# A load that waits for seven eighths of the store ahead of it, and stores cut 56 to 8, in a scaled residual add

## The chip, the core and the metric

The kernel runs on one core of a Trainium2 chip. A core has a matrix engine (TensorE, PE in the profile), a vector engine (VectorE, DVE), a scalar engine, GpSimd (POOL) and SyncE (SP), which here only issues transfers and waits. Each engine works through its own list of instructions in order; semaphores tie the lists together. Data is moved between the main memory (HBM) and the on-chip memory (SBUF, 128 partitions) by 16 DMA engines. The metric is the device time of one launch in microseconds (us). The time before is 152.25 us, the median of 3 runs (152.24 to 152.48).

## The reference

```python
B, S, D = 512, 32, 640          # x, fx: (512, 32, 640) bf16, alpha: (1,) bf16

def reference(x, fx, alpha):
    return x + alpha * fx
```

Each of x, fx and the output has 10,485,760 elements of two bytes, 20.97 MB. So 41.94 MB are read and 20.97 MB are written.

## The kernel before

Each tensor is seen as 128 partitions of 81,920 contiguous elements. A partition's row is counted in units of K = 512 elements (1 KB), so a tensor is 160 units wide, and one unit over all partitions is 131,072 bytes. The row is worked through in three pieces (line 18): units 0 to 64, 64 to 128 and 128 to 160. They are called p0, p1 and p2; the parts of fx, x and the output that belong to them are f0, x0 and the first store; f1, x1 and the second store; f2, x2 and the third.

On the chip there are three slots of 64 units each, a, b and c (line 42). f0 goes to slot a, x0 to b, f1 to c. x1 goes to slot a again, once f0 has been used up, and f2 and x2 share slot b (lower and upper half), once the first store has read it.

The order is written out by hand (`manual_schedule`, line 40): each engine does its work in the order of the lines, and the framework adds only the waits that the data needs. All transfers, loads and stores alike, are issued by SyncE in `move` (lines 45 to 48), so they go through one queue in the order of the calls: f0's first 8 units, its other 56, alpha, x0, f1, the first store, x1, f2, x2, the second store, the third. The three waits on that list that matter here are these. The first store (line 87) waits for its addition. x1's load (line 88) needs slot a, which the addition on line 85 has read by then, so it is issued right behind the first store. f2 (line 90) needs slot b and so waits until the first store has landed; x2 follows it at once.

VectorE does two kinds of steps, in place. `scaled` (line 61) multiplies a piece of fx by alpha, which a small matrix product has spread over the 128 partitions (lines 73 to 80); `added` (line 64) adds the scaled piece to the piece of x. Its order is: scale f0, add into x0, scale f1, add into x1, scale f2, add into x2. Each addition of a 64-unit piece is one instruction, and the store behind it waits for the whole of it.

The last instruction on SyncE (lines 97 to 100) waits for everything but the third store.

Of the kernel before, what the change touches and what calls it, by code (L numbers as in the profile page):

```python
# [1 line left out]

# [4 lines left out]

ALU = mybir.AluOpType
F32 = mybir.dt.float32

K = 512
P = 128

WIDE = 64
PIECES = [(0, 64), (64, 128), (128, 160)]
HEAD = 8


@with_exitstack
def kernel(
    ctx: ExitStack,
    tc: tile.TileContext,
    x: bass.AP,
    fx: bass.AP,
    alpha: bass.AP,
    out: bass.AP,
):  # L30
    nc = tc.nc
    xv = x.flatten_outer_dims().rearrange("(p n) d -> p (n d)", p=P)
    fxv = fx.flatten_outer_dims().rearrange("(p n) d -> p (n d)", p=P)
    ov = out.flatten_outer_dims().rearrange("(p n) d -> p (n d)", p=P)
    assert xv.shape[1] == PIECES[-1][1] * K

    consts = ctx.enter_context(tc.tile_pool(name="consts", bufs=1))
    psum = ctx.enter_context(tc.tile_pool(name="psum", bufs=1, space=bass.MemoryType.PSUM))
    slots = ctx.enter_context(tc.tile_pool(name="slots", bufs=1))
    ctx.enter_context(tc.manual_schedule())  # L40

    slot = [slots.tile([P, WIDE * K], x.dtype, name=f"slot_{n}") for n in "abc"]
    done = []

    def move(out, in_):
        r = nc.sync.dma_start(out=out, in_=in_)  # L46
        done.append(r)
        return r

    def load(of, piece, at, cut=0):  # L50

        a, b = piece
        n, where = at
        t = slot[n][:, where * K : (where + b - a) * K]
        if cut:
            move(t[:, : cut * K], of[:, a * K : (a + cut) * K])
        move(t[:, cut * K :], of[:, (a + cut) * K : b * K])
        return t

    def scaled(f):  # L60
        done.append(nc.vector.tensor_scalar(out=f, in0=f, scalar1=a_f[:], scalar2=None, op0=ALU.mult))  # L61

    def added(xt, f):
        done.append(nc.vector.tensor_tensor(out=xt, in0=xt, in1=f, op=ALU.add))  # L64

    def store(piece, t):
        a, b = piece
        move(ov[:, a * K : b * K], t)

    p0, p1, p2 = PIECES  # L70
    f0 = load(fxv, p0, (0, 0), cut=HEAD)

    a_1 = consts.tile([1, 1], alpha.dtype, name="a_1")
    move(a_1[:], alpha[None, :])
    ones = consts.tile([1, P], alpha.dtype, name="ones")
    nc.vector.memset(ones[:], 1.0)  # L76
    a_ps = psum.tile([P, 1], F32, name="a_ps")
    done.append(nc.tensor.matmul(a_ps[:], ones[:], a_1[:], start=True, stop=True))  # L78
    a_f = consts.tile([P, 1], F32, name="a_f")
    nc.vector.tensor_copy(out=a_f[:], in_=a_ps[:])  # L80

    x0 = load(xv, p0, (1, 0))
    scaled(f0)
    f1 = load(fxv, p1, (2, 0))
    added(x0, f0)
    scaled(f1)
    store(p0, x0)
    x1 = load(xv, p1, (0, 0))
    added(x1, f1)
    f2 = load(fxv, p2, (1, 0))  # L90
    x2 = load(xv, p2, (1, WIDE // 2))
    scaled(f2)
    store(p1, x1)
    added(x2, f2)
    store(p2, x2)

    rest = nc.sync.nop(nofuse=True)
    info = mybir.DependencyInfo(mybir.DependencyClass.Sync, mybir.DependencyReason.DATA)
    for i in done[:-1]:
        tc.add_manual_dep(rest.ins, i.ins.name, info, reason="all but the last store")  # L100


# [1 line left out]
_INS = ['x', 'fx', 'alpha']  # L104
_OUTS = [((512, 32, 640), 'bfloat16')]


# [23 lines left out]
```

## Time and profile before

| | us |
|---|---|
| time, median of 3 runs | 152.25 |
| the profiled run | 152.39 |
| its span in the profile | 150.6 |
| VectorE busy | 65.4 (43% of the span) |
| addition over 64 units | 17.22 |
| scaling of 64 units | 8.75 |
| addition over 32 units | 8.69 |
| scaling of 32 units | 4.48 |
| a SyncE issue | 0.33 to 0.52 |

The span is the time from the first to the last instruction of the profiled execution; the run's own time has 1.79 us around it. The page counts 1442 DMA packets and 62.92 MB, a mean of 418 GB/s over the span. VectorE's waits before a step are 10.2 us for x0, 2.1 for f1 and 31.8 for x1.

Three views are used below. The timeline gives start and length of each instruction, its engine, line and operands, and in brackets how long its engine had been idle and what ended that. A transfer stands in it only with its issue on SyncE; the table of issues has the time from there to landing, which is when all 16 engines have reported the end. In the table of windows, each line is one stretch: its bounds, its length, the busy time and number of instructions of PE, PEld, DVE and POOL, the granted clock of TensorE, the DMA share (the summed time of the packets that start in the stretch, over 16 times its length) and the GB/s of those packets. As a packet is booked whole where it starts, a short stretch can have a share over 1. A packet here is what one engine moves of one partition's row, so 65,536 bytes for a piece of 64 units, 8192 for 8 units.

### The profile page before, as it was taken

Reading aid. Unit: us, or ns where it says so; the run is one execution under the profiler, and the core shown is the slowest. Engines: PE = TensorE matmul, PEld = TensorE weight load, DVE = VectorE, ACT = ScalarE, POOL = GpSimd, SP = SyncE. Lnnn points to the kernel's source line nnn. Section 1 sums busy time; section 2 is a strip of 40 time slices with the busy share of each in tenths; the row PEclk is TensorE's granted clock in tenths of the full one; section 3 lists DMA queues with packets and bytes.
Section 4 is the critical chain, followed back from the end, with each engine's and each line's share of the span. In section 5 each row is a group of like instructions: output and inputs, shape, how many; then the busy total and the mean of one; then the engine's idle time right before and its main releaser. Section 6 shows DMA issues by size and latency. Waiting matters only on the chain.

```text
span 150.6 us, 74 instructions
## 1 busy us (share of the span) xinstructions
PE 0.2 (0%) x1; PEld 0.1 (0%) x1; DVE 65.4 (43%) x8; POOL 0.2 (0%) x4
## 2 busy tenths in 40 slices
PE   0000000000000000000000000000000000000000
PEld 0000000000000000000000000000000000000000
DVE  0000009930099996895000000009999999900000
POOL 0000000000000000000000000000000000000000
DMA  5995996998969696998978999979999969898993
GB/s 174 592 487 244 487 522 278 557 470 366 557 278 557 278 557 278 557 487 348 557 278 348 470 435 418 470 331 418 426 435 435 548 278 557 366 470 383 435 418 157
DMA packets 1442, 62.92 MB, mean 418 GB/s; under 512 B 162, under 2 KB 162, under 8 KB 162
## 3 DMA queue, kind: packets, MB, share of 16 engines
q1 hardware_dynamic: 1442, 62.92, 97.6%
HBM read 41.94 MB, written 20.97 MB: 418 GB/s over the span
## 4 chain that ended last, share of the span: by engine, by line
DMA 54%; DVE 27%; issue 5%; SPq 1%; DVEq 0%
DMA slot_a<-in_x_dram 28%; DMA slot_b<-in_x_dram 26%; DVE slot_b L64 17%; DVE slot_a L64 6%; DVE slot_b L61 3%; SPq L46 1%; DVEq L64 0%
## 5 line engine op out<-in xcount | busy, mean ns | idle before, releaser
L64 DVE TENSOR_TENSOR slot_a<-slot_a,slot_c 128x32768 bf16<-128x32768 bf16 x1 | 17.2, 17224 | 31.8 <-DMA slot_a<-in_x_dram 31.8
L64 DVE TENSOR_TENSOR slot_b<-slot_b,slot_a 128x32768 bf16<-128x32768 bf16 x1 | 17.2, 17224 | 10.2 <-DMA slot_b<-in_x_dram 10.2
L61 DVE TENSOR_SCALAR slot_c<-slot_c,a_f 128x32768 bf16<-128x32768 bf16 x1 | 8.8, 8754 | 2.1 <-DMA slot_c<-in_fx_dram 2.1
L80 DVE COPY a_f<-a_ps 128x1 f32<-128x1 f32 x1 | 0.2, 159 | 21.5 <-PE a_ps L78 21.5
L61 DVE TENSOR_SCALAR slot_a<-slot_a,a_f 128x32768 bf16<-128x32768 bf16 x1 | 8.8, 8754 | 0.0
L64 DVE TENSOR_TENSOR slot_b<-slot_b 128x16384 bf16<-128x16384 bf16 x1 | 8.7, 8693 | 0.0
L61 DVE TENSOR_SCALAR slot_b<-slot_b,a_f 128x16384 bf16<-128x16384 bf16 x1 | 4.5, 4479 | 0.0
L76 DVE MEMSET ones<- 1x128 bf16 x1 | 0.2, 165 | 0.8 <-PEq L115 0.8
L78 PE MATMUL a_ps<-a,ones 1*128 1x1 bf16 x1 | 0.2, 158 | 22.3 <-DMA a<-in_alpha_dram 22.3
L115 POOL MEMSET const-bfloat16-1.0<- 128x1 bf16 x1 | 0.1, 101 | 0.0
L115 POOL MEMSET const-uint8-127<- 128x1 uint8 x1 | 0.1, 101 | 0.0
L78 PEld LDWEIGHTS <-ones 1*128 1x128 bf16 x1 | 0.1, 100 | 1.0 <-DVE ones L76 1.0
L115 POOL MEMSET const-float32-0.0<- 128x1 f32 x1 | 0.1, 98 | 0.2 <-issue 0.2
L115 POOL MEMSET const-float32-1.0<- 128x1 f32 x1 | 0.1, 98 | 0.0
## 6 DMA issues: line engine op xcount, KB each, us to landing
slot_a<-in_fx_dram SPq DMA_DIRECT2D x1, 7168.0 KB, 21.0
slot_b<-in_fx_dram SPq DMA_DIRECT2D x1, 4096.0 KB, 29.9
slot_b<-in_x_dram SPq DMA_DIRECT2D x1, 4096.0 KB, 39.3
out_dram<-slot_b SPq DMA_DIRECT2D x1, 4096.0 KB
slot_a<-in_fx_dram SPq DMA_DIRECT2D x1, 1024.0 KB, 4.6
a<-in_alpha_dram SPq DMA_DIRECT2D x1, 0.0 KB
slot_b<-in_x_dram SPq DMA_DIRECT2D x1, 39.5
slot_c<-in_fx_dram SPq DMA_DIRECT2D x1, 58.5
```

The source lines that it names most:

```text
L46: r = nc.sync.dma_start(out=out, in_=in_)
L61: done.append(nc.vector.tensor_scalar(out=f, in0=f, scalar1=a_f[:], scalar2=None, op0=ALU.mult))
L64: done.append(nc.vector.tensor_tensor(out=xt, in0=xt, in1=f, op=ALU.add))
L76: nc.vector.memset(ones[:], 1.0)
L78: done.append(nc.tensor.matmul(a_ps[:], ones[:], a_1[:], start=True, stop=True))
L80: nc.vector.tensor_copy(out=a_f[:], in_=a_ps[:])
L115: nc = _bacc.Bacc("TRN2", target_bir_lowering=False, num_devices=1)
```

## The change

The order of the steps moves from calls to a text, `PLAN`, which a loop reads line by line; the three slots become one tile, `room`, whose places are given in units (0, 64 and 128 are the old slots a, b and c). `f` and `x` are loads and `s` is a store, each with the units in the tensor and, after `@`, the place in `room`; `a` spreads alpha; `m` scales, with place and width; `+` adds, with the places of x and f and the width. `room` is 207 units wide, of which 192 are used.

Three things differ in what is issued. The first store goes as units 0 to 56 and 56 to 64. x1's load has an added wait: it is issued when the first of these two stores has landed. The addition into x1 and the second store go as 56 and 8 units. f2's load follows x1's with no wait of its own, and x2's waits for the second part of the first store, whose place it takes. Pieces, places, the order of the loads and VectorE's order are otherwise those of before.

```diff
-WIDE = 64
-PIECES = [(0, 64), (64, 128), (128, 160)]
-HEAD = 8
+PLAN = """
+f 0 8 @ 0
+f 8 64 @ 8
+a
+x 0 64 @ 64
+m 0 64
+f 64 128 @ 128
++ 64 0 64
+m 128 64
+s 0 56 @ 64
+s 56 64 @ 120
+x 64 128 @ 0 after s 0
++ 0 128 56
++ 56 184 8
+f 128 160 @ 64
+x 128 160 @ 96
+m 64 32
+s 64 120 @ 0
+s 120 128 @ 56
++ 96 64 32
+s 128 160 @ 96
+"""
...
+    def transfer(what, a, b, at, after):
+        away, here = units(whole[what], a, b), units(room, at, at + b - a)
+        out, in_ = (away, here) if what == "s" else (here, away)
         r = nc.sync.dma_start(out=out, in_=in_)
+        if after:
+            tc.add_manual_dep(r.ins, moved[after].ins.name, info, reason="issued late")
+        moved[what, a] = r
         done.append(r)
...
-    p0, p1, p2 = PIECES
-    f0 = load(fxv, p0, (0, 0), cut=HEAD)
...
-    x0 = load(xv, p0, (1, 0))
-    scaled(f0)
-    f1 = load(fxv, p1, (2, 0))
-    added(x0, f0)
-    scaled(f1)
-    store(p0, x0)
-    x1 = load(xv, p1, (0, 0))
-    added(x1, f1)
-    f2 = load(fxv, p2, (1, 0))
-    x2 = load(xv, p2, (1, WIDE // 2))
-    scaled(f2)
-    store(p1, x1)
-    added(x2, f2)
-    store(p2, x2)
```

More of the change, by code (lines that the diff above doesn't have):

```diff
@@ L12 @@
 P = 128
-WIDE = 64
-PIECES = [(0, 64), (64, 128), (128, 160)]
-HEAD = 8
+ROOM = 207
+PLAN = """
[20 more added lines that the diff above has]
+"""
 @with_exitstack
@@ L31 @@
     nc = tc.nc
[L32 to L35, printed above, removed]
+    whole = {
+        name: t.flatten_outer_dims().rearrange("(p n) d -> p (n d)", p=P)
+        for name, t in (("x", x), ("f", fx), ("s", out))
+    }
+    assert whole["x"].shape[1] == 160 * K
     consts = ctx.enter_context(tc.tile_pool(name="consts", bufs=1))
@@ L38 @@
     psum = ctx.enter_context(tc.tile_pool(name="psum", bufs=1, space=bass.MemoryType.PSUM))
-    slots = ctx.enter_context(tc.tile_pool(name="slots", bufs=1))
+    rooms = ctx.enter_context(tc.tile_pool(name="rooms", bufs=1))
     ctx.enter_context(tc.manual_schedule())
-    slot = [slots.tile([P, WIDE * K], x.dtype, name=f"slot_{n}") for n in "abc"]
-    done = []
-    def move(out, in_):
+    room = rooms.tile([P, ROOM * K], x.dtype, name="room")
+    a_f = consts.tile([P, 1], F32, name="a_f")
@@ new lines, with units, spread_alpha @@
+    info = mybir.DependencyInfo(mybir.DependencyClass.Sync, mybir.DependencyReason.DATA)
+    done, moved = [], {}
+    def units(t, a, b):
+        return t[:, a * K : b * K]
+    def spread_alpha():
+        a_1 = consts.tile([1, 1], alpha.dtype, name="a_1")
+        done.append(nc.sync.dma_start(out=a_1[:], in_=alpha[None, :]))
+        ones = consts.tile([1, P], alpha.dtype, name="ones")
+        nc.vector.memset(ones[:], 1.0)
+        a_ps = psum.tile([P, 1], F32, name="a_ps")
+        done.append(nc.tensor.matmul(a_ps[:], ones[:], a_1[:], start=True, stop=True))
+        nc.vector.tensor_copy(out=a_f[:], in_=a_ps[:])
@@ L46, in move @@
+    def transfer(what, a, b, at, after):
+        away, here = units(whole[what], a, b), units(room, at, at + b - a)
+        out, in_ = (away, here) if what == "s" else (here, away)
         r = nc.sync.dma_start(out=out, in_=in_)
+        if after:
+            tc.add_manual_dep(r.ins, moved[after].ins.name, info, reason="issued late")
+        moved[what, a] = r
         done.append(r)
[L48 to L68, printed above, removed]
-    p0, p1, p2 = PIECES
-    f0 = load(fxv, p0, (0, 0), cut=HEAD)
-    a_1 = consts.tile([1, 1], alpha.dtype, name="a_1")
-    move(a_1[:], alpha[None, :])
-    ones = consts.tile([1, P], alpha.dtype, name="ones")
@@ L76 @@
[L76 to L80, printed above, removed]
-    x0 = load(xv, p0, (1, 0))
-    scaled(f0)
-    f1 = load(fxv, p1, (2, 0))
-    added(x0, f0)
-    scaled(f1)
-    store(p0, x0)
-    x1 = load(xv, p1, (0, 0))
-    added(x1, f1)
-    f2 = load(fxv, p2, (1, 0))
-    x2 = load(xv, p2, (1, WIDE // 2))
@@ L92 @@
-    scaled(f2)
-    store(p1, x1)
-    added(x2, f2)
-    store(p2, x2)
-    rest = nc.sync.nop(nofuse=True)
-    info = mybir.DependencyInfo(mybir.DependencyClass.Sync, mybir.DependencyReason.DATA)
+    for step in PLAN.strip().split("\n"):
+        what, *rest = step.split()
+        if what == "a":
+            spread_alpha()
+        elif what == "m":
+            t, n = map(int, rest)
+            f = units(room, t, t + n)
+            done.append(
+                nc.vector.tensor_scalar(out=f, in0=f, scalar1=a_f[:], scalar2=None, op0=ALU.mult)
+            )
+        elif what == "+":
+            t, u, n = map(int, rest)
+            xt, f = units(room, t, t + n), units(room, u, u + n)
+            done.append(nc.vector.tensor_tensor(out=xt, in0=xt, in1=f, op=ALU.add))
+        else:
+            a, b, _, at = rest[:4]
+            after = (rest[5], int(rest[6])) if len(rest) > 4 else None
+            transfer(what, int(a), int(b), int(at), after)
@@ L99 @@
+    last = nc.sync.nop(nofuse=True)
     for i in done[:-1]:
-        tc.add_manual_dep(rest.ins, i.ins.name, info, reason="all but the last store")
+        tc.add_manual_dep(last.ins, i.ins.name, info, reason="all but the last store")
 _INS = ['x', 'fx', 'alpha']
```

## The prediction

> **What bounds the kernel now.** I read the page's queue part first, then the chain of waits, the SyncE timeline, and tables of short windows around the places where the queue changes from loads to stores or back.
>
> ```profile
> span 150.6 us, 74 instructions
> DVE  0000009930099996895000000009999999900000
> DMA  5995996998969696998978999979999969898993
> q1 hardware_dynamic: 1442, 62.92, 97.6%
> ```
>
> One queue carries everything, and its packets fill 97.6% of 16 engines' time; VectorE is idle in more than half of the slices. So a microsecond is gained only where the 16 DMA engines move less than they can, and not by VectorE.
>
> ```profile
> 0.73 0.86 SPq L46 DMA_DIRECT2D slot_a<-in_fx_dram  x2
> 58.91 0.35 SPq L46 DMA_DIRECT2D out_dram<-slot_b  x1
> 59.37 0.36 SPq L46 DMA_DIRECT2D slot_a<-in_x_dram  x1
> 60.95 8.75 DVE L61 TENSOR_SCALAR slot_c<-slot_c,a_f 128x32768 bf16<-128x32768 bf16 x1 [2.08 <-DMA slot_c<-in_fx_dram]
> 81.23 0.33 SPq L46 DMA_DIRECT2D slot_b<-in_fx_dram  x1
> 101.54 17.22 DVE L64 TENSOR_TENSOR slot_a<-slot_a,slot_c 128x32768 bf16<-128x32768 bf16 x1 [31.83 <-DMA slot_a<-in_x_dram]
> 118.79 0.34 SPq L46 DMA_DIRECT2D out_dram<-slot_a  x1
> ```
>
> This is the timeline (start, us, engine, line). Landings follow from it and from the issue table's times to landing: f0 1.17 + 21.0 = 22.2, f1 2.40 + 58.5 = 60.9, the first store at 81.2 (SyncE was waiting for it and issues at 81.23), x1 at 101.44 (59.37 + 42.07 in the chain), x2 81.60 + 39.3 = 120.9, the second store 118.79 + 21.4 = 140.2. Between landings 64 units take 38.7/2 = 19.35 us over x0 and f1 (22.2 to 60.9), 19.5 for f2 and x2, 19.3 for the second store; but the first store and x1 together take 101.44 - 60.9 = 40.5, against 2 x 19.35 = 38.7. **1.8 us are lost where the first store turns into a load**, and nothing returns them. Short windows (us, busy engines, clock, DMA share, GB/s; a packet is booked where it starts) show the place:
>
> ```profile
> 72.00:73.00 1.00, 0.00 (x0) 0.00 (x0) 0.00 (x0) 0.00 (x0) 1.00 2.42 1049
> 77.00:78.00 1.00, 0.00 (x0) 0.00 (x0) 0.00 (x0) 0.00 (x0) 1.00 3.00 1049
> 80.00:82.00 2.00, 0.00 (x0) 0.00 (x0) 0.00 (x0) 0.00 (x0) 1.00 1.35 524
> 82.00:83.00 1.00, 0.00 (x0) 0.00 (x0) 0.00 (x0) 0.00 (x0) 1.00 1.13 459
> ```
>
> 1049 GB/s over 1 us is 16 packets of 65,536 bytes, one per engine. At 72 they took 2.42 us each; the store's last 16, begun at 77, took 3.00, and x1's first 16 (524 GB/s over 2 us), begun at 80 to 82, took 2.70; seven at 82 took 1.13 x 16/7 = 2.58. The mean engine lost 0.58 + 0.28 + 0.07 = 0.93 us, the slowest, which sets the landing, the 1.8. DVE and SyncE are idle there. Where loads turn into a store nothing of the kind is seen (x2 to the second store: 19.3). So reading x1 from HBM begins while the store still writes to HBM, and both suffer.
>
> This fits a rule of the Trainium skill, "DMA: Bandwidth & Descriptors", section "Two DMAs through the same engine are not ordered": descriptors start in order, but an engine's read and write sides are separate, so a later one can be read while an earlier is still written. By it alone, what counts is whether x1's descriptors are there when the read side is done with the store, which is case A below.
>
> **The change, part by part.** (1) *x1 waits for 7/8 of the store.* SyncE now stands at the x1 issue until s 0 56 has landed; behind it stand f2, x2 (which waits for s 56 64 besides) and the second store. What runs meanwhile: s 56 64, eight 8 KB packets per engine. Their price is that of the head of f0:
>
> ```profile
> 1.65:3.20 1.55, 0.00 (x0) 0.00 (x0) 0.00 (x0) 0.00 (x0) 1.00 0.99 291
> 3.20:4.20 1.00, 0.00 (x0) 0.00 (x0) 0.00 (x0) 0.00 (x0) 1.00 0.99 418
> ```
>
> From 3.2 to 4.2 us 418 KB are 51 packets in 0.99 x 16 us: 0.31 each, eight 2.48 us. Is that cover long enough? How late a landing is reported, and how soon an issue brings packets, the seams around both stores show:
>
> ```profile
> 60.20:60.70 0.50, 0.00 (x0) 0.00 (x0) 0.00 (x0) 0.00 (x0) 1.00 4.90 2097
> 119.30:119.60 0.30, 0.00 (x0) 0.00 (x0) 0.30 (x1) 0.00 (x0) 1.00 0.01 0
> 119.60:119.85 0.25, 0.00 (x0) 0.00 (x0) 0.25 (x1) 0.00 (x0) 1.00 7.40 3146
> ```
>
> The first store's 16 first packets (2097 x 0.5 = 1049 KB) start between 60.2 and 60.7, as f1's last ones end, and f1 lands at 60.9: 0.7 us after the first engine was through, 0.2 or more after the last. SyncE wakes in 0.02 (the first store landed at 58.91 + 22.3 = 81.21). The second store, issued at 118.79, starts on 12 engines (3146 x 0.25 = 786 KB) between 119.60 and 119.85: 0.81 to 1.06 us. So x1 reaches the first engine 2.48 - 0.7 - 0.02 - (0.81 to 1.06) = 0.7 to 0.95 us before it runs dry, the last one 1.2 to 1.45. No gap, and f2 (issued some 0.4 behind x1) has 19 us of cover. x2 waits for s 56 64, about 3 us on, and also has x1 ahead of it.
>
> What the late issue does to the seam, no row shows. Bounds: it keeps the whole loss (1.8), or it leaves only what a load pays that starts on idle engines. That is the head of f0, in the first of the two lines above: 451 KB, 55 packets, took 0.99 x 1.55 x 16 = 24.6 us, at 0.31 each it would be 17.1: 7.5/16 = 0.5 us lost per engine. As a limit from outside, nothing lost at all. x1's descriptors are no longer there 18 us ahead but about 1 us ahead, and the packet that the reads run into is 8 KB long instead of 64. Both shorten the overlap, neither removes it: I take the middle of 0.5 and 1.8, 1.2, a gain of 0.6; the ends of the gain are 1.8 and 0.
>
> (2) *The stores as 56 and 8.* Twice eight packets of 0.31 in place of one of 2.42: 2 x 0.06 = +0.12 us on the queue, the bound. Packets of 56 KB cost in proportion. Two more issues of 0.35 us lie on SyncE, which waits most of the time. Upper bound: each small store pays what f0's start paid, 0.5, so +1.0 on top; lower: 0.
>
> The Trainium skill's rule against such splitting, same page, section "Rules for kernel authors", asks for 1 MiB or more per DMA, and its bandwidth table gives 341 GB/s at that size: an estimate of 3.1 us for 8 units, +0.65 each, +1.3 in all. In this trace the 1024 KB head ran at 418 GB/s with the next transfer queued behind it.
>
> (3) *The second add as 56 and 8.* 17.22 x 7/8 = 15.07, then 2.15 and at most 0.1 between them. The second store is issued 15.1 us after x1 lands instead of 17.3. Before, 12 engines had finished x2 and waited for it; but the last engine had not: x2 landed at 120.9 and the store 19.3 later, at full rate. The end is set by that engine, so 0 (bounds 0 and -0.3, what the waits between 119.3 and 119.6 show). Scaling f2 and the last add (4.48 + 8.69) end some 31 us after x1 lands, near 131.5, and the second store runs until 139: 8 us of cover.
>
> **Sum.** -0.6 + 0.12 + 0 = -0.5 us on the profiled run: span 150.1, and with the 1.79 around it (152.39 - 150.6) 151.9. That run is 0.14 above the median 152.25, so 151.75; rounded 151.7.
>
> **Rivals.**
> *A, the seam costs what it did.* For it: x1 still arrives 0.7 us or more before the store ends, and an engine's read side needs no more. Against: the store's last 64 KB packet was slow on all 16 engines. Price: +0.12, 152.4.
> *B, x1 comes too late (slower).* If a store's landing is reported later than a load's, the cover is eaten: it decides from 0.7 us of extra delay on. At 1.3 us extra the first engine is dry for 0.5, and since engines run dry one by one, those reading still disturb those writing and the 1.8 stays: 152.25 + 0.12 + 0.5 = 152.9. Against it: the first store's landing at 81.2 falls within the 80 to 82 in which x1's first packets start, no later than f1's did.
> *C, small stores are dear.* +1.0 by the cold start, on an unchanged seam: 152.25 + 0.12 + 1.0 = 153.4, on the gained one 152.8. Against it: the 0.31 above; but that was a load, and no small store is in the trace.
> *D, the late issue clears the seam.* It leaves 0.5 or nothing: -1.3 to -1.8, with +0.12 at 150.6 to 151.1. It is the far end of the forecast's mechanism.
>
> **Chances.** Forecast (151.1 to 151.95) 0.34, D 0.17, A (151.95 to 152.55) 0.22, B 0.18, C 0.09. What a measurement of this kernel can tell from no change is 0.2%, 0.3 us. Forecast and D are faster: 0.51; A is same: 0.22; B and C slower: 0.27. The range leaves out the fastest part of D and C with the worst of B: 150.8 to 152.9. The faster cases alone span 150.6 to 151.95.
>
> **What would show it.** Right: x1 lands some 40.0 us after f1 (38.7 + 1.2 + 0.06), the store's last and x1's first packets take less extra than 0.58 + 0.28 us, no window between them lacks packets. The second store is issued near 116. Small packets in the seam at 0.31 and a landing of s 0 56 near 77.8 (60.9 + 7/8 x 19.35) confirm parts 1 and 2. Wrong: windows near 79 to 80 with no starts (B); small store packets above 0.4 us (C); x1 landing at 101.5 again (A).

## The result, and the profile after

The changed kernel takes 153.7 us (median of 5 runs, 153.03 to 154.1), against 152.48 for the kernel before measured beside it (152.24 to 152.87). The ratio is 1.0088, 95% interval 1.0063 to 1.0112: it is slower by about 1.3 us. 151.7 had been forecast, with a range of 150.8 to 152.9, so the time lies above the range.

The head of the page after, and its queue:

```profile
span 152.2 us, 79 instructions
DMA  5996999996969989699969799989999999979990
q1 hardware_dynamic: 1730, 62.92, 96.8%
```

The profiled run took 153.95 us, 1.56 more than that of before (152.39). The 16 engines still have packets nearly all the time, so the loss is in how long packets take, or in engines that no longer end together. The timeline (start, us, engine, line, operands, idle time before; a line with x2 or x3 groups that many instructions, and its time runs from the start of the first to the end of the last):

```profile
59.08 0.82 SPq L90 DMA_DIRECT2D out_dram<-room  x2
61.14 8.75 DVE L104 TENSOR_SCALAR room<-room,a_f 128x32768 bf16<-128x32768 bf16 x1 [2.09 <-DMA room<-in_fx_dram]
78.25 0.34 SPq L90 DMA_DIRECT2D room<-in_x_dram  x1
80.68 0.33 SPq L90 DMA_DIRECT2D room<-in_x_dram  x1
101.60 17.30 DVE L109 TENSOR_TENSOR room<-room 128x28672 bf16<-128x28672 bf16 x2 [31.70 <-DMA room<-in_x_dram]
116.72 15.66 SPq L90 DMA_DIRECT2D out_dram<-room  x3
```

f1 lands at 61.1, x1 is issued at 78.25 and lands at 101.5 (78.25 + 23.3, its time to landing): 40.4 us after f1, against 40.5 before. The seam around x1 costs what it did. The second store's first part is issued at 116.72, 2.07 us earlier than before, as worked out. But x2, issued at 80.68, lands 41.7 later at 122.4: **20.9 us after x1, against 19.5 before**. What follows, nearly 30 us of stores, takes as long as it did. So 1.4 of the 1.56 us arise at the end of x2. Windows there (bounds, length, busy engines, clock, DMA share, GB/s), first of before, then of after:

```profile
111.00:116.00 5.00, 0.00 (x0) 0.00 (x0) 5.00 (x1) 0.00 (x0) 1.00 1.02 439
116.00:119.00 3.00, 0.00 (x0) 0.00 (x0) 3.00 (x2) 0.00 (x0) 1.00 0.91 393
```

```profile
111.00:116.00 5.00, 0.00 (x0) 0.00 (x0) 5.00 (x1) 0.00 (x0) 1.00 1.02 439
116.00:119.00 3.00, 0.00 (x0) 0.00 (x0) 3.00 (x3) 0.00 (x0) 1.00 1.02 360
```

A packet of f2 or x2 has 32,768 bytes. Between 116 and 119 us 393 x 3 = 1179 KB are 36 packets of before, each taking 0.91 x 3 x 16/36 = 1.21 us; after, 1080 KB are 33 packets of 1.02 x 3 x 16/33 = 1.48 us on average. Up to 116 both run at the same rate. x2's last packets are slowed as soon as the second store can be in the queue behind them. VectorE is busy in both.

The seam between the first store and x1, after:

```profile
77.20:79.30 2.10, 0.00 (x0) 0.00 (x0) 0.00 (x0) 0.00 (x0) 1.00 0.94 390
79.30:79.90 0.60, 0.00 (x0) 0.00 (x0) 0.00 (x0) 0.00 (x0) 1.00 1.04 369
79.90:81.10 1.20, 0.00 (x0) 0.00 (x0) 0.00 (x0) 0.00 (x0) 1.00 2.46 881
```

Until 79.3 the small packets take 0.94 x 2.1 x 16/100 = 0.32 us (390 x 2.1 = 819 KB, 100 packets), so small stores are as cheap as the head of f0. The next 27 take 0.37, and from 79.9 on x1's 16 first packets (with one small one: 881 x 1.2 = 1057 KB) take 2.93 in place of 2.42. No window is empty. The delay has moved from the store's packets to x1's. It has become smaller for the mean engine, (27 x 0.06 + 16 x 0.51)/16 = 0.6 us in place of 0.93, but the landing, which the slowest engine sets, came only 0.1 us sooner after f1.

### The profile page after: what moved, and what is told of

Its sections match the earlier page's. It is cut to its first block, busy times and chain, and to the rows that moved or that the text cites. A ratio compares the mean times of both kernels' runs of the same rounds, so it can differ in the third digit from the quotient of the medians.

```text
span 152.2 us, 79 instructions
## 1 busy us (share of the span) xinstructions
PE 0.2 (0%) x1; PEld 0.1 (0%) x1; DVE 65.4 (43%) x9; POOL 0.2 (0%) x4
## 4 chain that ended last, share of the span: by engine, by line
DMA 65%; DVE 20%; SPq 1%; issue 0%; DVEq 0%
DMA room<-in_x_dram 51%; DVE room L109 17%; DMA out_dram<-room 14%; DVE room L104 3%; SPq L90 1%; SPq L80 0%; DVEq L109 0%
## 5 line engine op out<-in xcount | busy, mean ns | idle before, releaser
L109 DVE TENSOR_TENSOR room<-room 128x32768 bf16<-128x32768 bf16 (+3 forms) x4 | 43.2, 10824 | 42.2 <-DMA room<-in_x_dram 42.1
L104 DVE TENSOR_SCALAR room<-room,a_f 128x32768 bf16<-128x32768 bf16 (+1 forms) x3 | 22.0, 7329 | 2.1 <-DMA room<-in_fx_dram 2.1
## 6 DMA issues: line engine op xcount, KB each, us to landing
room<-in_x_dram SPq DMA_DIRECT2D x1, 4096.0 KB, 41.7
out_dram<-room SPq DMA_DIRECT2D x1, 4096.0 KB, 19.4
```

## The experiments

In all runs below the landings are read as in the prediction: f1 from the step of VectorE that waits for it, x1 and x2 from the start of their issues and the table's times to landing. "Above before" is the ratio to the kernel before in the same session.

### First four: which part costs

The edits of the first three are against the changed kernel's plan, that of the fourth is against the second of them.

The late x1 alone:

```diff
-+ 0 128 56
-+ 56 184 8
++ 0 128 64
-s 64 120 @ 0
-s 120 128 @ 56
+s 64 128 @ 0
```

> The change without its part on the second store: the first store goes as 56 and 8 and x1 waits for the 56, but the second add and the second store are whole. Theory 'early store' (the second store, issued 2 us earlier, disturbs x2's last packets): x2 lands some 19.5 us after x1 as before, time within 0.4 us of before. Theory 'skew' (the late x1 leaves the engines further apart and x2 suffers from that): x2 lands 20.5 us or more after x1, time 1 us or more above before. Theory 'small stores' (8 KB store packets are dear): half of the loss, +0.6.

The second split alone (x1 at once, first store whole):

```diff
-s 0 56 @ 64
-s 56 64 @ 120
-x 64 128 @ 0 after s 0
+s 0 64 @ 64
+x 64 128 @ 0
```

> The kernel before with the second add and the second store alone cut to 56 and 8; x1 is issued at once behind a whole first store. 'Early store': x2 lands 20.5 us or more after x1 and the time is 1.0 to 1.6 us above before. 'Skew': time as before. 'Small stores': +0.6.

The second add whole, with both stores still 56 and 8:

```diff
-+ 0 128 56
-+ 56 184 8
++ 0 128 64
```

> The change with the second add whole again, so that the second store's two parts (56 and 8) are issued when the whole add is done, near 118.8. 'Early store': x2 lands 19.5 us after x1, time within 0.5 us of before, of which 0.12 are the small packets. 'Small stores' or 'skew': time as the changed kernel, 1.2 above before.

The second add and store as halves, again with x1 at once and the first store whole (against the second split alone):

```diff
-+ 0 128 56
-+ 56 184 8
++ 0 128 32
++ 32 160 32
-s 64 120 @ 0
-s 120 128 @ 56
+s 64 96 @ 0
+s 96 128 @ 32
```

> The kernel before with the second add and store cut 32 and 32, no 8 KB store packets; the first half is issued near 110, some 10 us before x2 is done. 'Early store', paid once at the seam: like the 56 and 8 cut, 1.0 to 1.6 us above before, x2's packets at full rate until its last one or two. If a waiting store disturbs loads as long as it waits, x2's packets are slow from 111 on and the time is 3 us or more above before. 'Small stores': time as before.

| | ratio to before, interval | x1 after f1, us | x2 after x1, us |
|---|---|---|---|
| changed kernel | 1.0088 (1.0063 to 1.0112) | 40.4 | 20.9 |
| late x1 alone | 1.0033 (1.0020 to 1.0046) | 40.4 | 19.4 |
| second split alone | 1.0053 (1.0039 to 1.0068) | 40.2 | 20.1 |
| second add whole | 1.0035 (1.0021 to 1.0049) | 40.4 | 19.8 |
| second in halves | 1.0075 (1.0054 to 1.0096) | 40.3 | 20.3 |

The two parts add up: 0.33% + 0.53% = 0.86%, of the 0.88% measured. The larger part is the early second store: when it is issued at 116.7 (second split) or 110.3 (halves), x2 lands late, and when it is issued at 119 with the very same small packets (second add whole), nearly all of that is gone and the time is that of the late x1 alone. So neither the small store packets nor engines further apart are needed for the loss, as the theories "small stores" and "skew" had it. The second split alone reached 0.8 us rather than the 1.0 to 1.6 expected. In the profiles it sets x2 back by 0.6 us (20.1 against 19.5), and together with the late x1 by 1.4; whether the late x1 makes it worse, one profile of each can't tell, and the medians add up without that.

In the run with halves the store's first part is issued at 110.3 and waits in the queue:

```profile
111.00:116.00 5.00, 0.00 (x0) 0.00 (x0) 5.00 (x1) 0.00 (x0) 1.00 1.02 439
116.00:119.00 3.00, 0.00 (x0) 0.00 (x0) 3.00 (x2) 0.00 (x0) 1.00 1.04 328
```

Up to 116 us x2 moves at 439 GB/s, as in the kernel before; then 30 packets take 1.04 x 3 x 16/30 = 1.66 us on average. The loss is paid once, at the change from loads to the store, and not as long as the store waits.

### Next four: the control, and what the seam is

The late x1 alone was still 0.33% above before. Its control is the kernel before written as a plan (whole stores and adds, x1 at once). Beside it ran two ways of issuing x1 later still, and the first store issued early. The edits of these three against that control, in the order of the table:

```diff
 s 0 64 @ 64
-x 64 128 @ 0
+x 64 128 @ 0 after s 0
...
-s 0 64 @ 64
-x 64 128 @ 0
+s 0 60 @ 64
+s 60 64 @ 124
+x 64 128 @ 0 after s 0
...
-+ 64 0 64
++ 64 0 56
++ 120 56 8
 m 128 64
-s 0 64 @ 64
+s 0 56 @ 64
+s 56 64 @ 120
```

> The kernel before, written as the plan of the changed kernel (one tile of 207 units in place of three slots, same places, same order, whole stores, x1 issued at once). Theory 'late x1 costs' (the 0.5 us of the run with the late x1 alone come from the wait or its small packets): time as before, within 0.2 us. Theory 'frame' (they come from the new frame, before the first store is even issued): 0.3 to 0.5 us above before, f1 landing at 61.2 instead of 60.9, and everything after f1 as long as before.

> As the kernel before in the plan's form, but x1 is issued when the whole first store has landed, so that no load is in the queue while that store moves. Theory 'overlap' (packets ahead of a change of direction are slowed by the descriptors queued behind them): the store's last 16 packets take 2.42 us, the queue is empty for about 1.3 us, x1 pays 0.5 on starting, lands 40.2 to 40.6 us after f1 and within 0.6 us over all engines instead of 1.5. Theory 'HBM turn-around' (writing then reading costs, however far apart): the same 0.9 us per engine and the 1.3 of emptiness on top, 41.5 or more.

> As the late x1 alone, with the first store cut 60 and 4 units: the cover is 8 packets of 4 KB, 1.3 us, so x1's first packets come as the store ends or 0.2 us later. 'Overlap': the store's packets stay undisturbed, x1 pays little more than 0.5, lands 39.6 to 40.0 after f1, time 0.5 us under the late x1 alone. 'HBM turn-around': 40.4 or more after f1, time as the late x1 alone.

> The kernel before in the plan's form with the first add and the first store cut 56 and 8, so that the first store is issued near 57.0 instead of 59.1, while two of f1's packets per engine are to come; the engines stand within 0.3 us of each other here. 'Early store': f1's last packets are slow as x2's were in the split second store, f1 lands 0.5 us or more later, near 61.8. If x2's loss needs engines that stand 1.5 us apart ('skew'): f1 lands at 61.2 as in the other plan runs, no slow packets.

| | ratio to before, interval | f1 lands, us | x1 after f1, us |
|---|---|---|---|
| before as a plan | 1.0008 (0.9994 to 1.0021) | 61.3 | 40.3 |
| x1 after the whole store | 1.0105 (1.0092 to 1.0119) | 61.2 | 41.8 |
| x1 after 15/16 | 1.0035 (1.0018 to 1.0051) | 61.2 | 40.3 |
| first store early | 0.9964 (0.9952 to 0.9976) | 62.3 | 38.7 |

The frame is not the cause. Its profile shows f1 at 61.3, as that theory said, but its time is that of before.

The run with x1 behind the whole store speaks against the reading of the seam that the prediction used:

```profile
77.00:78.00 1.00, 0.00 (x0) 0.00 (x0) 0.00 (x0) 0.00 (x0) 1.00 2.42 1049
79.40:81.20 1.80, 0.00 (x0) 0.00 (x0) 0.00 (x0) 0.00 (x0) 1.00 0.01 0
81.20:82.50 1.30, 0.00 (x0) 0.00 (x0) 0.00 (x0) 0.00 (x0) 1.00 2.51 807
```

With no load in the queue the store's last 16 packets take 2.42, undisturbed. Then no data packet starts for 1.8 us (an engine stands still for about 2 us, where 1.3 had been expected: the store's last packets start between 77.15 and 77.85, x1's first between 81.60 and 82.50), and x1's 16 first packets (807 x 1.3 = 1049 KB) take 2.51 x 1.3 x 16/16 = 3.26 us, 0.84 above 2.42. The kernel before lost 0.93 over store and x1 together. So a load that starts on an empty queue pays nearly the whole loss with nothing else moving, more than the 0.5 that "overlap" allowed. This run by itself doesn't show that the seam's loss is the same one, and part of its 41.8 us is the longer standstill. But x1 after 15/16 gained nothing either, so both late issues fell on the side of the theory "HBM turn-around".

But that theory doesn't hold either, since the first store issued 2 us early did away with the seam's loss, although x1 was in the queue behind it long before its end, which "overlap" took to be the cause. f1 lands a microsecond later there, as "early store" said, and then the store and x1 together take 38.7 us, the 2 x 19.35 of undisturbed transfers. It is faster than before by 0.36%, which no theory had expected.

### Last four: the reading ahead

A third theory fits the seams of all eight runs. An engine reads ahead of what it writes. It keeps that lead as long as the next transfer's descriptors (the entries of the queue that it works off) are there when its reading gets to them. If the store at the end of the loads comes too late for that, the lead is gone, which costs next to nothing where the store starts (its first packets took 4.90 x 0.5 = 2.45 us in the kernel before); but the next load from HBM must build it up again, at the 0.6 to 0.9 us per engine seen at the seams. If the store comes early the lead is kept, at a price at the end of the loads, and the next load starts free. This is inferred: no view shows reading and writing of an engine apart. These runs were chosen so that it could fail. The edits are against the plan's form of before:

```diff
-s 0 64 @ 64
+s 0 56 @ 64
+s 56 64 @ 120
...
-+ 64 0 64
++ 64 0 56
++ 120 56 8
-s 0 64 @ 64
-x 64 128 @ 0
+s 0 56 @ 64
+s 56 64 @ 120
+x 64 128 @ 0 after s 0
...
-+ 64 0 64
++ 64 0 32
++ 96 32 32
-s 0 64 @ 64
+s 0 32 @ 64
+s 32 64 @ 96
...
-+ 64 0 64
++ 64 0 60
++ 124 60 4
-s 0 64 @ 64
+s 0 60 @ 64
+s 60 64 @ 124
```

> The kernel before in the plan's form with the first store cut 56 and 8 but the first add whole, so that both parts are issued near 59.3; x1 is issued at once behind them. Theory 'read lead' (an engine's reading runs ahead of its writing as long as the queue always holds the next descriptors before reading gets there; where it has to start again from HBM it costs 0.6 to 0.9 us per engine, and a store that comes late at the end of the loads lets the lead go): seam from the store to x1 as before, x1 40.2 to 40.5 us after f1, time within 0.2 us of the plan's form of before. Theory 'small packets free the seam' (in the run with the early first store it was the eight small packets ahead of x1 that made its seam cheap): x1 39.0 after f1, time 0.8 us below.

> As the early first store (first add and store cut 56 and 8), but x1 waits for the first part as in the changed kernel. 'Read lead': the queue again holds nothing behind the small store when reading gets there, so the seam's loss of 0.8 per engine is back, on top of the 0.7 at f1's end: x1 40 us or more after f1, time 0.8 to 1.3 us above the early first store. 'Small packets free the seam': as the early first store.

> First add and first store cut 32 and 32, x1 at once: no 8 KB packets, the first half issued near 50.6. 'Read lead': f1's end loses 0.6 to 0.9 us per engine as with the 56 and 8 cut, the seam to x1 nothing (x1 38.7 to 39.0 after f1), time as the early first store within 0.3 us. 'Small packets free the seam': the seam loses 0.9 as well, time 1 us or more above the early first store.

> First add and first store cut 60 and 4, x1 at once: the first part is issued near 58.2, its packets come at 59.1, some 1.5 us before f1 is done. 'Read lead': either reading of f1 has ended by then and the result is as before (no loss at f1, 0.9 at the seam to x1), or not, and it is as the early first store; in both cases the two losses do not come together. A time 0.3 us or more below the early first store would mean that the lead can be kept without paying at f1.

| | first store issued, us | ratio to before, interval | f1 lands, us | x1 after f1, us |
|---|---|---|---|---|
| cut 56 and 8, add whole | 59.3 | 1.0006 (0.9992 to 1.0021) | 61.3 | 40.1 |
| 60 and 4 | 58.1 | 0.9941 (0.9919 to 0.9962) | 61.2 | 39.0 |
| 56 and 8 (above) | 57.2 | 0.9964 (0.9952 to 0.9976) | 62.3 | 38.7 |
| 56 and 8, x1 late | 57.1 | 1.0056 (1.0035 to 1.0077) | 62.2 | 40.3 |
| halves | 50.8 | 0.9974 (0.9961 to 0.9987) | 62.2 | 38.7 |

The small packets do not free the seam (first row: 40.1), and without any 8 KB packets it is free (last row: 38.7). With the early store and the late x1 both losses are paid, here f1's last packets and x1's first:

```profile
57.90:58.50 0.60, 0.00 (x0) 0.00 (x0) 0.60 (x1) 0.00 (x0) 1.00 5.10 1638
80.50:82.00 1.50, 0.00 (x0) 0.00 (x0) 0.00 (x0) 0.00 (x0) 1.00 2.06 754
```

1638 x 0.6 = 983 KB are 15 packets of 5.10 x 0.6 x 16/15 = 3.26 us. 754 x 1.5 = 1131 KB are x1's 16 first packets and ten small ones; with 0.31 for a small one, x1's took (2.06 x 1.5 x 16 - 10 x 0.31)/16 = 2.90, so 0.5 is lost there rather than the 0.8 expected. That is the clearest sign against the idea behind the late issue: the one added wait takes the gain of the early store away and brings the ratio to the kernel before from 0.9964 to 1.0056, 1.4 us, a little more than the 0.8 to 1.3 expected.

What an early store costs at the end of f1 is seen in one window, 57.90 to 58.50, in which f1's last 16 packets start. In this order: before as a plan, 60 and 4, 56 and 8, halves, one line from each trace.

```profile
57.90:58.50 0.60, 0.00 (x0) 0.00 (x0) 0.60 (x1) 0.00 (x0) 1.00 4.05 1748
```

```profile
57.90:58.50 0.60, 0.00 (x0) 0.00 (x0) 0.60 (x2) 0.00 (x0) 1.00 4.22 1748
```

```profile
57.90:58.50 0.60, 0.00 (x0) 0.00 (x0) 0.60 (x1) 0.00 (x0) 1.00 5.13 1748
```

```profile
57.90:58.50 0.60, 0.00 (x0) 0.00 (x0) 0.60 (x1) 0.00 (x0) 1.00 5.57 1748
```

1748 x 0.6 = 1049 KB, 16 packets; the share times 0.6 is the time of one: 2.43, 2.53, 3.08, 3.34 us. And x1's packets after the halves, in a short window where ten of them start (1638 x 0.4 = 655 KB):

```profile
80.85:81.25 0.40, 0.00 (x0) 0.00 (x0) 0.00 (x0) 0.00 (x0) 1.00 3.80 1638
```

3.80 x 0.4 x 16/10 = 2.43 us each: nothing lost, where x1 on the empty queue paid 3.26.

The cut at 60 and 4 takes both: the store is issued 1.2 us before the time of the control, f1's packets pay 0.1, and x1 comes 39.0 after f1. x1's first packets are nearly undisturbed:

```profile
79.40:81.20 1.80, 0.00 (x0) 0.00 (x0) 0.00 (x0) 0.00 (x0) 1.00 1.74 726
```

726 x 1.8 = 1307 KB are 16 packets of 65,536 bytes and 63 of 4096; with 0.16 us for a small one, x1's took (1.74 x 1.8 x 16 - 63 x 0.16)/16 = 2.50. The theory had foreseen either no loss at f1 and the whole loss at the seam, or the other way round. Here both nearly vanish, which the expectation had named only as a further possibility (the lead kept without paying at f1), and the theory doesn't say why it should be so. The 151.42 us of this run (151.05 to 151.86) are the fastest median of the study, 0.6% under the kernel before and 1.5% under the changed one; its interval just overlaps that of 56 and 8. That it is a window of issue times, with its best near 58.1, is read from four points and wasn't searched further. Only the two runs cut 56 and 8 (59.3 and 57.2) differ in the time of the issue and not in the size of the parts as well.

## Why the prediction was wrong

**The bound was right.** The differences between the runs are read in the times of the transfers, and the 1.8 us lost between the first store and x1 were real: three runs recover them, or nearly (x1 38.7 or 39.0 after f1), two of them at a price of about 1 us at f1's landing.

**Step (3) failed.** The earlier second store was put at 0, bounds 0 and -0.3, because the engine that ends last had not waited for it, and the others would only wait less. Only the wait was priced, not what a waiting store does to the loads ahead of it. The row used, x2 and then the second store at full rate, was that of a store which comes just as the loads run out. The earlier store slows x2's last packets from 1.21 to 1.48 us on average and sets x2 back by 1.4 us in the profiled run; alone it costs 0.53%, 0.8 us. By the theory above, the lead that the early store keeps buys nothing here, since no load follows. Of the three times at which the second store was issued (110, 117 and 119) that of before is the cheapest. With +0.8 for 0 the forecast's sum is +0.3 in place of -0.5: this term alone turns the sign.

**Step (1) failed in its gain.** Of the 0.6 us taken, nothing came: x1 landed 40.4 us after f1, case A, and the part alone is 0.33% above before. The reason was wrong as well. I took the loss to be an overlap that a later issue would shorten. But a load in the queue behind an early store disturbs nothing (x1 38.7 us after f1), and issuing x1 late behind that store brings the loss back. A restart of reading, the theory above, fits this; it is inferred and not seen. The lower bound of 0.5, from f0's start on idle engines, was the right kind of row, but it is the loss of the mean engine and was set against the 1.8 of the slowest. The mean engine lost 0.93, so the two differ by 0.4, and a start on the empty queue then measured 0.84, which leaves next to no gain. The 0.4 us by which the late x1 is slower than its control (1.0033 against 1.0008, two sessions whose intervals just touch) stay open. The small packets aren't it (cut 56 and 8 with x1 at once: 1.0006), and in the profile of that run, the fastest of its eight, no stretch shows it.

**Step (2) was right.** Small store packets took 0.32 us until x1 came, and the cut alone cost 0.06%, which its interval doesn't tell from nothing. Case C fell with it. So did the estimate of +1.3 us from the bandwidth table of the Trainium skill, "DMA: Bandwidth & Descriptors", section "Bandwidth": 341 GB/s at 1 MB, where the small store moved 390 GB/s with the queue full. The 1 MiB that the rule asks for is just what 8 units are, so the rule, unlike the table, didn't speak against the cut; and the fastest run has a part of half that size.

**The cover was right, so case B was wrong.** s 0 56 had landed by 78.25 (expected near 77.8, with f1 0.2 later than before), and no window lacks packets. The slower side came from the second store, for which there was no rival: the cases looked at the first seam and at the price of small packets.

**The rule on separate read and write sides** (the Trainium skill, "DMA: Bandwidth & Descriptors", section "Two DMAs through the same engine are not ordered") bears on this case, though no run here shows the two sides apart. The conclusion from it was incomplete. If reading runs ahead, it counts whether descriptors are there when reading gets to them, and this holds for the store behind the loads too, not only for x1 behind the store.

## What to carry to other kernels

In a kernel bound by one queue of transfers, look at each change from loads to stores or back, and price it by the time of the last and first packets there. In this kernel a store that is followed by another load was worth issuing a little before the loads ahead of it ran out, 1.2 us earlier; a store that no load follows was best issued just as they ran out. Holding a load back so that it doesn't meet a store gained nothing at 7/8, at 15/16 or behind the whole store, and cost 0.3% to 1.05%.

## What was not expected

- A load that starts on an empty queue paid 0.84 us per engine on its first packets (3.26 against 2.42), when all 16 engines began within 1 us of each other and nothing else moved.
- A store waiting behind loads slows only their last packets: with the store in the queue for 5 us, x2 still moved 439 GB/s, and then its packets took 1.66 us on average in place of 1.21.
- Cutting a store into 60 and 4 units with its add, so that it is issued 1.2 us sooner, was worth 0.9 us in a kernel whose DMA engines were already 97.6% busy.
